# Five instead of eight filler matmuls between the taps' transposes and the first h in a fused convolution and feed-forward kernel

## The chip, the cores and the metric

The kernel runs on one core of a Trainium2 chip. The metric is the device time in microseconds (us), the median of three runs. Engines are named as in the profile: PE is TensorE's matrix multiply and PEld its weight load, DVE is VectorE, ACT is ScalarE, POOL is GpSimd, SP is the engine whose queue issues most of the DMAs (SPq in the rows); ACTq is ScalarE's DMA queue. L12 is line 12 of the kernel.

## The reference

Two layers, each a gated long convolution followed by a feed-forward block, on 2048 rows of 512 values in bfloat16. Cut to what is computed:

```python
def _A_ref(q, k, v, shift_k, ssm_k, ssm_D):      # S = 2048, D = 512, ks = 4
    k_shift = sum over t of k_pad[:, t:t + S, :] * shift_k[:, ks - 1 - t]   # 4 taps
    kv = k_shift * v
    y = causal convolution of kv with ssm_k along S (written with FFTs of length 2 S)
    y = y + kv * ssm_D
    return q * y

def _B_ref(x, w_gate, w_up, w_down):             # F = 1792
    return (silu(x @ w_gate) * (x @ w_up)) @ w_down

x = A_q
for layer in (0, 1):
    x = x + _A_ref(_layernorm(x), A_k, A_v, A_shift_k, A_ssm_k, A_ssm_D)
    x = x + _B_ref(_layernorm(x), B_w_gate, B_w_up, B_w_down)
```

## The kernel before

The 2048 rows are cut into four blocks of 512 rows, and a block into R = 4 residues of 128. The long convolution is done with short spectra made by matmul: a block of the filter (`hn`, the tensor `A_ssm_k`, called h) is transposed on PE into `hs` (`transpose_h`, L489), multiplied by a table of cosines and sines `fwd` (`half`, through `mm` at L323) and copied out of PSUM as `ev` and `G`. A block of k is transposed on PE (`transpose_k`, L378), shifted by the four taps with diagonal matrices `dg` (`shift_mul`, through L323), multiplied by v, and turned into the spectrum `X` (`direct`, L470). Products of spectra come back through a table `inv` (L809). The feed-forward block multiplies by `wg_sb` and `wu_sb` (L323, tile `pf`) and by `wd_sb` (L994, tile `pd`).

Nothing is scheduled at run time. Every operation is added to a plan with an engine, an estimated cost, and the buffers it reads and writes. A table written out by hand, ORDER, gives the one order in which all operations are issued; each engine executes its own instructions in that order. `Plan.order` computes an estimated start and end for each operation from the costs, and the PSUM or SBUF slot of each buffer. PSUM slots come in three rings, `pf` (4 slots), `pc` (2) and `pd` (2). Real waits are semaphores, put in by the framework where a buffer written by one instruction is used by another, or a slot is used again.

`Plan.issue` walks through the order and emits the instructions. Ahead of a PE operation that by the estimate begins over 0.5 us after the PE operation before it, and before 32 us, it emits filler matmuls: `warm` (L1307) multiplies a constant 128x128 matrix of ones by itself n times into a free PSUM slot, and nothing reads the outcome. In the profile they are the tile `wm`. The number is the estimated gap, less an allowance, divided by 0.106 us. There are three such places in the kernel before: 25 fillers at the very start, 8 between the taps' transposes and the transposes of h, and 2 much later, ahead of the spectrum of the second h.

The first operations of PE, in program order, are then:

- 25 fillers into a slot of ring `pf`.
- four tiny transposes of the taps (`turn_taps`, L1173), into a slot of ring `pd`; the first waits for the DMA of `tapR`, issued on ACT's queue (L1107).
- 8 fillers into slot 0 of ring `pf`.
- 16 transposes of h (L489), four for each residue. The first weight load waits for the DMA of `hn`, which is the first on SP's queue (L354); the first transpose itself waits for a semaphore of PE, since it writes the PSUM slot that the last filler wrote.
- 12 transposes of k (L378); the first weight load waits for the DMA of `kn`, the second on SP's queue (L364).
- the first spectrum matmuls on `hs` and `fwd`, and so on.

DVE copies residue 0 of h into `hs`, adding the row `drow` (L502), and residue 1 (L505); ACT copies residues 2 and 3 (L499). Each waits for four of PE's transposes.

Of the kernel before, what the change touches and what calls it, by code (L numbers as in the profile page):

```python
# [140 lines left out]
class Plan:  # L141
# [78 lines left out]
    def issue(self, seq, place, when, warm_until, warm):  # L220
        t, busy = 0.0, {}
        for o in seq:
            start, end = when[o]
            if o.eng == "PE":
                if start < warm_until and start - t > 0.5:
                    for ring, i in [(r, i) for r in ("pf", "pd", "pc") for i in range(self.rings[r])]:
                        if busy.get((ring, i), 0.0) <= t:
                            n = int((start - t - (0.0 if 0.0 < t < 8.0 else 0.3)) / 0.106)
                            if n > 0:
                                warm(ring, i, n)  # L230
                            break
                t = end
            for b in o.bufs:
                if b.t is None:
                    b.slot = place.get(b, 0)
                    b.t = b.make(b.slot)
                if b in place:
                    busy[b.ring, place[b]] = max(when[q][1] for q in b.ops) + 0.2
            o.emit()
# [1101 lines left out]
```

## Time and profile before

| what | us |
|---|---|
| median of three runs (343.62 to 343.71) | 343.68 |
| time of the profiled execution | 343.72 |
| its span, from the first to the last instruction | 341.9 |
| PE busy in the span | 337.6 |
| DVE busy | 282.5 |
| ACT busy | 252.5 |
| POOL busy | 37.0 |

The profiled execution spends 1.8 us outside the span. Times in the rows of the timeline and of the chain are counted from the span's start; a row of the timeline gives start, duration, engine, line, operation and tiles, and how many instructions of one kind in sequence it stands for, with the idle time before them in brackets. The ends of matmuls are modelled, and matmuls overlap, so what one costs PE is read from the distance between starts, not from its duration.

### The profile page before, as it was taken

What the parts mean: (1) busy time and instruction counts of PE and PEld (TensorE: products, weight loads), DVE (VectorE), ACT (ScalarE), POOL (GpSimd) and SP (SyncE); (2) the same over time, 40 slices, a digit from 0 to 9 for tenths busy, and PEclk for the clock granted to TensorE, in tenths of its full rate; (3) what the DMA queues carried; (4) which work ended last, traced back from release to release, by engine and by line L of the source; (5) the groups of instructions that cost most, each with busy time, mean ns of one, the idle gap of its engine ahead of it and who ended that gap; (6) DMA issues with size and microseconds to landing.
All of it is one profiled execution on the core that took longest, in us unless ns stands there. A gap on an engine that the chain in (4) does not pass through costs nothing.

```text
span 341.9 us, 6474 instructions
## 1 busy us (share of the span) xinstructions
PE 337.6 (99%) x2566; PEld 243.4 (71%) x2566; DVE 282.5 (83%) x478; ACT 252.5 (74%) x496; POOL 37.0 (11%) x46
## 2 busy tenths in 40 slices
PE   9999999999999999999999999999999999999996
PEld 7656858668686567768587756768685877777683
DVE  8899999999999999999999999889997433726022
ACT  6999999999977475778999963778665545545451
POOL 4000100102106100103200000101101000001000
PEclk9999999999999999999999999999999999999999
DMA  7999314050325164010110223010102100001011
GB/s 262 342 314 350 55 31 63 0 155 1 34 46 94 31 124 140 3 30 2 33 31 3 48 46 125 0 33 1 33 0 49 32 33 0 15 17 31 17 33 31
DMA packets 42088, 22.95 MB, mean 67 GB/s; under 512 B 33989, under 2 KB 39882, under 8 KB 42058
## 3 DMA queue, kind: packets, MB, share of 16 engines
q1 hardware_dynamic: 41904, 22.49, 26.1%
q8 instruction: 20, 0.33, 0.4%
q14 instruction: 10, 0.08, 0.1%
q10 hardware_dynamic: 154, 0.05, 0.1%
HBM read 12.33 MB, written 2.10 MB: 42 GB/s over the span
## 4 chain that ended last, share of the span: by engine, by line
PE 93%; ACT 3%; DVE 1%; DMA 1%; issue 0%; POOL 0%; POOLq 0%; ACTq 0%
PE pf L323 56%; PE pd L994 27%; PE ps L323 6%; PE ps L470 2%; DMA zT<-z 1%; ACT H L431 1%; PE wm L1307 1%; PE pt L489 1%; ACT Yk L729 1%; ACT ks L526 0%; ACT n L874 0%; DVE bnst L821 0%; ACT Yk L703 0%; PE pt L378 0%; DVE xc L902 0%
## 5 line engine op out<-in xcount | busy, mean ns | idle before, releaser
L323 PE MATMUL pf<-zT,wu_sb 128*128 128x256 bf16 (+1 forms) x872 | 110.0, 275 | 0.4 <-DMA zT<-z 0.3
L323 PE MATMUL pf<-zT,wg_sb 128*128 128x256 bf16 (+1 forms) x872 | 110.3, 276 | 0.0
L994 PE MATMUL pd<-wd_sb,ht 128*128 128x512 bf16 (+1 forms) x462 | 106.2, 373 | 0.0
L323 PEld LDWEIGHTS <-wu_sb 128*128 128x128 bf16 x872 | 85.2, 98 | 19.5 <-DMA zT<-z 0.8
L323 PEld LDWEIGHTS <-wg_sb 128*128 128x128 bf16 x872 | 85.3, 98 | 17.3
L977 ACT CAST ht<-pf 128x512 bf16<-128x512 f32 x112 | 64.8, 590 | 23.7 <-PE pf L323 23.4
L974 ACT ACTIVATE sg<-pf 128x512 bf16<-128x512 f32 x112 | 66.3, 603 | 20.7 <-PE pf L323 17.3
L994 PEld LDWEIGHTS <-ht 128*128 128x128 bf16 x462 | 45.1, 98 | 44.1
L979 DVE TENSOR_TENSOR ht<-ht,sg 128x1024 bf16<-128x1024 bf16 (+1 forms) x61 | 38.8, 640 | 20.4 <-ACT ht L977 14.3
L826 POOL TENSOR_TENSOR rstd<-ve,nhalf 128x2 f32<-128x2 f32 x24 | 25.1, 1046 | 193.1 <-DVE ve L824 193.1
L821 DVE BATCH_NORM_STATS2 bnst<-xc 128x6 f32<-128x512 bf16 x48 | 31.8, 684 | 0.5
L1075 ACT CAST dn<-pd 128x512 bf16<-128x512 f32 x30 | 17.2, 588 | 17.5 <-PE pd L994 17.5
L431 ACT ACTIVATE X<-ps 128x512 bf16<-128x512 f32 x32 | 18.9, 606 | 10.5 <-PE ps L323 10.0
L1078 DVE TENSOR_TENSOR xc<-xc,dn 128x1024 bf16<-128x1024 bf16 x15 | 10.3, 686 | 16.8 <-ACT dn L1075 16.8
L669 DVE TENSOR_TENSOR t<-X,G 128x2048 bf16<-128x2048 bf16 x18 | 21.9, 1217 | 0.1
L665 DVE TENSOR_TENSOR t<-X,G 128x2048 bf16<-128x2048 bf16 x18 | 21.9, 1219 | 0.0
L855 POOL TENSOR_TENSOR rstd<-ve,nhalf 128x2 f32<-128x2 f32 x8 | 8.4, 1048 | 79.3 <-ACT ve L853 79.3
L679 DVE TENSOR_TENSOR Z<-Z,t 128x2048 bf16<-128x2048 bf16 x12 | 14.7, 1221 | 0.3
L677 DVE TENSOR_TENSOR t<-t,t 128x2048 bf16<-128x2048 bf16 x12 | 14.6, 1219 | 0.2
L431 ACT ACTIVATE H<-ps 128x512 bf16<-128x512 f32 x24 | 14.1, 611 | 0.0
L901 DVE TENSOR_TENSOR n<-n,Yk 128x1024 bf16<-128x1024 bf16 x15 | 10.3, 689 | 3.2 <-ACT n L874 1.9
L323 PE MATMUL ps<-hs,fwd 128*128 128x512 bf16 x40 | 12.7, 379 | 0.1
(103 smaller groups left out, 322.4 us busy)
## 6 DMA issues: line engine op xcount, KB each, us to landing
hn<-in_A_ssm_k_dram SPq DMA_DIRECT2D x4, 512.0 KB, 5.9
vt<-in_A_v_dram SPq DMA_DIRECT2D x4, 512.0 KB, 6.4
xc<-in_A_q_dram SPq DMA_DIRECT2D x4, 512.0 KB, 5.3
out_dram<-xc SPq DMA_DIRECT2D x15, 128.0 KB, 1.8
wg_sb<-in_B_w_gate_dram SPq DMA_DIRECT2D x1, 1792.0 KB
wu_sb<-in_B_w_up_dram SPq DMA_DIRECT2D x1, 1792.0 KB, 8.3
wd_sb<-in_B_w_down_dram SPq DMA_DIRECT2D x1, 1280.0 KB, 11.8
kn<-in_A_k_dram SPq DMA_DIRECT2D x1, 512.0 KB, 4.3
```

Source lines behind the costliest of these rows:

```text
L323: nc.tensor.matmul(o, lhsT=lhsT, rhs=rhs, start=(n == 0), stop=(n == len(terms) - 1))
L431: add("ACT", act(D), lambda: nc.scalar.activation(out=view(), in_=ps.t[:], func=ACT.Copy, scale=scale), r=[ps], w=[(buf, keys)], conv=conv)
L665: dve(n * D, lambda t1=t1, part=part: nc.vector.tensor_mul(out=t1.t[:], in0=x.t[:, sl, 0, :], in1=g.t[:, sl, part, :]), [(x, key(slots, (0 ...
L669: dve(n * D, lambda t2=t2, part=part: nc.vector.tensor_mul(out=t2.t[:], in0=x.t[:, sl, 1, :], in1=g.t[:, sl, 1 - part, :]), [(x, key(slots ...
L679: dve(n * D, lambda t1=t1, part=part: nc.vector.tensor_add(out=z.t[:, sl, part, :], in0=z.t[:, sl, part, :], in1=t1.t[:]), [t1], [zk], con ...
L821: add("DVE", 0.6, lambda st=st, i=i: nc.vector.bn_stats(out=st.t[:], in_=xs[c].t[:, i, :]), r=[(xs[c], (i,))], w=[st])
L826: add("POOL", pw, lambda: nc.gpsimd.tensor_tensor(out=rstd.t[:], in0=ve.t[:], in1=nhalf.t[:].to_broadcast((P, n)), op=ALU.pow), r=[ve, nha ...
L974: add("ACT", act(D), lambda ps=ps, sl=sl: nc.scalar.activation(out=sg.t[:, sl], in_=ps.t[:], func=ACT.Silu), r=[ps], w=[(sg, (b,))], due=( ...
L977: add("ACT", act(D), lambda ps=ps, sl=sl: nc.scalar.copy(out=ht.t[:, sl], in_=ps.t[:]), r=[ps], w=[(ht, (b,))], due=(us[0], at, 1.5, "a"))
L979: dve(n * m * W, lambda: nc.vector.tensor_mul(out=ht.t[:], in0=ht.t[:], in1=sg.t[:]), [sg], [ht], due=(us[0], (k + n) / NF, 0.0, "h"))
L994: nc.tensor.matmul((pds[o] if not cs.start else pds[HP]).t[:, cs], lhsT=ht.t[:, q, at, o * P:(o + 1) * P], rhs=wt["d"].t[:, ft, cs], start ...
L1075: add("ACT", act(D), lambda o=o: nc.scalar.copy(out=dn.t[:, o, :], in_=pds[o].t[:]), r=[pds[o]], w=[(dn, (o,))], due=(unit, 1.0, 3.0, "h"))
```

## The change

One constant in `Plan.issue`: where the operation before the gap ended, by the estimate, between 0 and 8 us, the allowance taken off the gap is 0.35 us instead of nothing. Only one of the three places falls in that range, the one between the taps' transposes and the first transpose of h. There the number of fillers goes from 8 to 5. In program order PE loses three weight loads and three matmuls of L1307 there; every other instruction of PE, and all those of DVE, ACT, POOL and SP, stand in the same order with the same waits. No buffer changes its slot.

```diff
@@ Plan.issue
                 if start < warm_until and start - t > 0.5:
                     for ring, i in [(r, i) for r in ("pf", "pd", "pc") for i in range(self.rings[r])]:
                         if busy.get((ring, i), 0.0) <= t:
-                            n = int((start - t - (0.0 if 0.0 < t < 8.0 else 0.3)) / 0.106)
+                            n = int((start - t - (0.35 if 0.0 < t < 8.0 else 0.3)) / 0.106)
                             if n > 0:
                                 warm(ring, i, n)
                             break
```

## The prediction

> **What bounds the kernel now.** I read the page first: its busy times, then the chain that ended last.
>
> ```profile
> span 341.9 us, 6474 instructions
> PE 337.6 (99%) x2566; PEld 243.4 (71%) x2566; DVE 282.5 (83%) x478; ACT 252.5 (74%) x496; POOL 37.0 (11%) x46
> PE 93%; ACT 3%; DVE 1%; DMA 1%; issue 0%; POOL 0%; POOLq 0%; ACTq 0%
> ```
>
> PE is busy nearly all the time and carries 93% of the chain. So any time that PE gains at the start can reach the end, if nothing between is tied to something that does not move. Next, the chain in order of time, cut to the start and to the places where it leaves PE (start, length, what):
>
> ```profile
> 0.76 2.83 PE wm L1307 x25
> 3.58 0.22 PE pt L1173 x4
> 3.81 0.98 PE wm L1307 x8
> 4.83 1.32 PE pt L489 x16
> 6.15 0.67 PE pt L378 x12
> ...
> 20.14 1.74 PE ps L470 x8
> 21.91 0.60 ACT X L431
> ...
> 31.91 0.62 ACT zT L940
> 32.58 1.91 PE pf L323 x16
> ...
> 261.15 4.00 DMA zT<-z
> 265.20 8.91 PE pf L323 x80
> ```
>
> The eight fillers lie on the chain, and the first transpose of h follows them with no DMA between. That is the important point: in this execution PE made h wait for the fillers, not the fillers for h. Whether h was there sooner is read from the start of its DMA, and from the distance of issue to landing:
>
> ```profile
> 0.72 0.46 SPq L354 DMA_DIRECT2D hn<-in_A_ssm_k_dram  x1
> hn<-in_A_ssm_k_dram SPq DMA_DIRECT2D x1, 512.0 KB, 3.5
> 1.24 0.49 SPq L364 DMA_DIRECT2D kn<-in_A_k_dram  x1
> kn<-in_A_k_dram SPq DMA_DIRECT2D x1, 512.0 KB, 4.3
> ```
>
> h landed at 0.72 + 3.5 = 4.22 us, give or take 0.05 for the rounding, and k at 1.24 + 4.3 = 5.54. The first transpose of h started at 4.83, 0.6 us after h was there.
>
> **The change step by step.** The timeline of PE around the place, with rows that narrow windows gave (start, length, count from that start on):
>
> ```profile
> 3.74 1.03 PE L1307 MATMUL wm<-const-bfloat16-1.0 128*128 128x128 bf16 x8
> 3.82 0.63 PE L1307 MATMUL wm<-const-bfloat16-1.0 128*128 128x128 bf16 x4
> 4.14 0.63 PE L1307 MATMUL wm<-const-bfloat16-1.0 128*128 128x128 bf16 x4
> 4.46 0.31 PE L1307 MATMUL wm<-const-bfloat16-1.0 128*128 128x128 bf16 x1
> 4.46 0.15 PEld L489 LDWEIGHTS <-hn 128*128 128x128 bf16 x1
> 4.83 1.32 PE L489 MATMUL pt<-ident,hn 128*128 128x128 bf16 x16
> 5.32 0.45 PE L489 MATMUL pt<-ident,hn 128*128 128x128 bf16 x4
> 5.42 0.39 PE L489 MATMUL pt<-ident,hn 128*128 128x128 bf16 x4
> 5.49 0.44 PE L489 MATMUL pt<-ident,hn 128*128 128x128 bf16 x5
> 5.54 0.39 PE L489 MATMUL pt<-ident,hn 128*128 128x128 bf16 x4
> 5.99 0.83 PE L378 MATMUL pt<-ident,kn 128*128 128x128 bf16 x12
> ```
>
> *What goes.* The second filler starts at 3.82 and the eighth at 4.46: (4.46 - 3.82) / 6 = 0.107 us each. Three fewer free 3 x 0.107 = 0.32 us. The fifth starts at 4.14 and, as long as the eighth, ends at 4.14 + 0.31 = 4.45. Before, the eighth ended at 4.46 + 0.31 = 4.77 and the first transpose began 0.06 later, which is its wait for PE's own semaphore. So now it can begin at 4.45 + 0.06 = 4.51.
>
> *What takes its place.* The weight load of h, which followed the eighth filler's without a wait, would follow the fifth's at 4.14 and now meet the DMA. In the chain, DMA zT ended at 261.15 + 4.00 = 265.15 and PE started at 265.20: 0.05 us from landing to start. So the load starts at about 4.22 + 0.05 = 4.27 (4.32 with the rounding) and takes 0.15: done at 4.42 to 4.47, just inside 4.51. The cover is thus 0.2 us if the matmul needs only the start of its load, and about 0.05 if it needs the end. Should h land later than this, each 0.1 us of it costs 0.1 us of the start, until at 0.32 us nothing is left of the gain.
>
> *What three fewer fillers are worth.* Not 0.32. The starts of the transposes go 5.32, 5.42, 5.49, 5.54: the distance falls from 0.107 to 0.056 at about 5.45. That is the clock of the array opening (the page's row of granted clock does not show it; the distances do). With the start at 4.51, three more transposes are done when the clock opens, and at the full clock three cost 3 x 0.056 = 0.17 us. If the clock opens at the same moment, or after the same number of matmuls of this size (25 fillers, 8 fillers and 7 transposes before; 25, 5 and 10 after, both ending at 5.42), all later work on PE begins 0.17 us sooner: the transposes of k at 5.82 instead of 5.99. k has landed by then (5.54 + 0.05 = 5.59), so this does not stop it: a margin of 0.23 us.
>
> [...]
>
> *What the other engines make of it.* The copies of h wait for PE, with all their idle time put down to the transposes:
>
> ```profile
> 5.45 0.42 DVE L502 TENSOR_TENSOR hs<-pt,drow 128x512 bf16<-128x512 bf16 x1 [0.42 <-PE pt L489]
> 5.74 1.07 ACT L499 COPY hs<-pt 128x512 bf16<-128x512 bf16 x2 [0.40 <-PE pt L489]
> ```
>
> DVE's first copy needs the fourth transpose, which comes 0.32 us sooner, and may start at 5.13; by its bracket DVE was idle from 5.45 - 0.42 = 5.03. ACT's needs the eighth, at 5.21 instead of 5.49, and may start at about 5.5; it was idle from 5.74 - 0.40 = 5.34. So both gain 0.2 us or more, and will not hold PE back. Of the queues, SP and POOL are moved past nothing; no DMA is issued sooner or later because of the fillers in this stretch.
>
> *Does it reach the end?* The table of stretches (us, then PE busy of it):
>
> ```profile
> 5.40:21.90 16.50, 16.50 (x159) 10.84 (x156) 15.23 (x32) 14.91 (x32) 2.56 (x5) 1.00 1.07 315
> 32.60:254.00 221.40, 221.40 (x1643) 160.74 (x1643) 215.13 (x326) 181.12 (x360) 26.44 (x23) 1.00 0.22 47
> ```
>
> PE has no idle time from 5.4 to 21.9, so 0.17 us is carried whole to 21.9. There the chain goes over to ACT: `X` at 21.91 begins just as the last matmul of 20.14 + 1.74 = 21.88 ends, so ACT's stretch to 32.5 begins 0.17 sooner too. From 32.6 to 254 PE is full again, and the transposing DMA at 261.15 follows from PE's and ACT's work, not from a fixed time. I find nothing on the chain after 6 us that stands still. What DMA brings by a fixed time (v, the weights, the tables) does not appear on it.
>
> The sum: the profiled execution 343.72 - 0.17 = 343.55; its time was 0.04 above the median of the runs, so about 343.5 for a median. The bounds of this term: nothing, if h lands 0.3 us later in other executions or a later stage takes the gain back; 0.32, if the earlier start of DVE and ACT counts rather than PE's. I take 0.17, since the two windows with no idle PE say that PE sets the pace. A change of 0.2%, 0.7 us, is about what a measurement of this kernel can tell from no change; 0.17 is far below.
>
> **The rivals.**
>
> *The clock opens later (slower).* The mechanism sits at 5.45 us. It decides if transposes count for less than fillers, and if the work seen until then is near the least that opens the clock. Before, 33 fillers had run by then; after, 30. If only work other than transposes counts, three matmuls of that size are missing, and the next to count are the spectrum matmuls that follow 16 + 12 transposes: at 0.107 us those 28 take 3.0 us from 4.51 on, so to 7.5, and one spectrum matmul of 512 columns (four times 0.107) makes up the rest: the clock opens at about 7.9. From 5.45 to 7.9 PE runs at half the pace and loses 2.45 / 2 = 1.2 us; less the 0.17 gained, +1.05: 344.7. The least is a delay of only the three fillers' 0.32 us, half of it lost, which just eats the gain. The most is that the whole waiting starts again at 5.45 for as long as it took from the first filler to the opening, 5.45 - 0.76 = 4.7 us: 2.35 lost, +2.2, 345.9. Since PE has no idle time until 21.9, nothing would hide it. Against it: the opening came in the middle of the transposes, 0.6 us after PE had gone over to them, which looks as if they count. For it: a window of fixed length could show the same. [...] Chance 0.30.
>
> *The gain does not arrive.* h lands later without the profiler or by chance, or one of the waits between 21.9 and 32.6 takes the 0.17 us back, since ACT and DVE are nearly full there. Then 343.7. For it: the cover of 0.05 to 0.2 us at the landing of h is thin. Against it: the chain. Chance 0.15.
>
> *More than forecast.* If the clock opened with the first transposes, PE would be at k's transposes at 5.59, where the landing of k stops it: 5.99 - 5.59 = 0.40 sooner, 343.3. Nothing speaks for an earlier opening. Beyond that no row has a gain of 0.7 us. Chance 0.10 in all, of which I leave 0.06 for a gain above 0.2% by something that these rows do not show.
>
> **How the numbers follow.** The forecast, 343.4 to 343.6, has 0.45, and with it goes the most likely value, 343.5. Within 0.2% lie the forecast, the case without gain and the smaller part of the third rival: 0.45 + 0.15 + 0.04 = 0.64. Slower is the first rival, 0.30. The range begins at 343.3 (the third rival's price) and must reach into the slower case to leave out only 2 in 10: to 344.9, which takes in 344.7 and leaves out the repeats of a whole wait. Its own range without the slower case would be 343.3 to 343.7.
>
> **What would show it.** In the profile of the changed kernel: five `wm` in the second group, the first transpose of h at 4.5, with its load at about 4.3 after a wait for the DMA; the step from 0.107 to 0.056 at 5.4 to 5.5, in the tenth or eleventh transpose; k's transposes at 5.8; and `X` on the chain at 21.7. I am wrong if the starts still lie 0.107 apart after 5.6, if h's load comes later than 4.5, or if the difference at 21.9 is not that at 5.99.

## The result and the profile after

The changed kernel took 342.98 us (median of ten runs, 342.88 to 343.64) against 343.97 for the kernel before in the same runs. The ratio is 0.9974, with a 95% interval of 0.9966 to 0.9982: faster by 0.6 to 1.2 us, where 0.17 was forecast. The profiled execution took 343.52 us with a span of 341.7, against 343.72 and 341.9 before. That is a gain of only 0.2, since these two executions started differently, as will be seen.

The start first. Three views of the changed kernel's PE: the weight loads of h, and the starts around the opening of the clock (start, length, count from there on).

```profile
4.46 0.78 PEld L489 LDWEIGHTS <-hn 128*128 128x128 bf16 x8 [0.28 <-DMA hn<-in_A_ssm_k_dram]
4.50 0.69 PE L489 MATMUL pt<-ident,hn 128*128 128x128 bf16 x5
...
6.27 0.47 PE L378 MATMUL pt<-ident,kn 128*128 128x128 bf16 x4
6.38 0.41 PE L378 MATMUL pt<-ident,kn 128*128 128x128 bf16 x4
6.46 0.39 PE L378 MATMUL pt<-ident,kn 128*128 128x128 bf16 x4
6.52 0.39 PE L378 MATMUL pt<-ident,kn 128*128 128x128 bf16 x4
```

The first transpose of h begins at 4.50, as forecast, its load after a wait for the DMA. But the starts are 0.11 us apart until 6.38 and 0.06 from 6.46 on: the clock opened at about 6.4, not 5.45, one microsecond later. So the work at 32 us is not ahead but behind: the first `pf` matmul stands at 32.88, against 32.58 on the chain before. Yet the execution ended 0.2 us sooner. So about 0.5 us must have been gained after 32 us. The chain in order of time, in the changed kernel, at the place where before it came from ACT, DVE and POOL to the transposing DMA at 261.15:

```profile
263.88 1.29 PE pd L994 x6
265.18 8.73 PE pf L323 x80
```

Now the chain stays on PE. (It counts the `pd` matmuls up to their modelled end at 265.18; the next matmuls start before that.) When `pf` really starts is in the timeline of PE, before and then after:

```profile
264.29 0.59 PE L994 MATMUL pd<-wd_sb,ht 128*128 128x512 bf16 x2
265.20 0.61 PE L323 MATMUL pf<-zT,wu_sb 128*128 128x256 bf16 x4 [0.32 <-DMA zT<-z]
```

```profile
264.37 0.81 PE L994 MATMUL pd<-wd_sb,ht 128*128 128x512 bf16 x3
265.01 0.82 PE L323 MATMUL pf<-zT,wu_sb 128*128 128x256 bf16 x6
```

Before, `pf` began at 265.20 because it had to wait for `zT`; now it begins at 265.01, without a wait, though PE was 0.3 us behind at 32 us. These 0.19 us are the 0.2 us by which the execution ended sooner.

The instructions on the tile `zT` between 261.0 and 262.2 us, first before, then after:

```profile
L908 SPq DMA_TRANSPOSE zT<-z x2: 1190/1224/1259, 259.9 to 261.2; - x2
DMA to landing us min/median/max: 2.4/3.2/4.0
```

```profile
L908 SPq DMA_TRANSPOSE zT<-z x2: 1198/1228/1257, 260.2 to 261.4; - x2
DMA to landing us min/median/max: 2.4/2.4/2.5
```

The same two DMAs: the second took 4.0 us to land before and 2.5 after. What lengthened it is read from the DMA queues, in narrow windows (queue and kind, packets that start in the window, MB, share of 16 engines; the share sets the packet's whole time against the window and says little here). Before, from 263.0 to 263.2, beside packets of the data queue q1:

```profile
q8 instruction: 1, 0.02, 32.3%
```

From 263.3 to 264.1 no packet starts at all, and then, from 264.1 to 264.2, the whole answer on queues is:

```profile
q1 hardware_dynamic: 2, 0.00, 2.8%
```

In the changed kernel from 262.0 to 265.0, the whole answer on queues, and then from 265.0 to 265.2:

```profile
q1 hardware_dynamic: 721, 0.25, 35.4%
...
q8 instruction: 1, 0.02, 30.0%
```

Queue q8 carries instructions. The page has 20 of its packets over the whole span, 0.33 MB, about one in 17 us. I take them to be PE's: the page has 5132 weight loads and matmuls for PE, a good 256 for each of the 20, and under 500 instructions for any other engine. In the trace before, one packet, 16 KB, ran from 263.09 to 264.12, while the second transposing DMA was under way: 15 of its 16 parts landed by 263.63, the last at 265.15. The two small packets above start at 264.11 and 264.12, as the instruction packet ends; 30 such packets had started by 263.3, two for each of the 15 parts that had landed. So the last part stood behind the instruction packet. After the change this packet comes at 265.14, when `zT` has landed (263.93). That gave theory F: the change takes six instructions out of PE's program, so that the fetches fall at other places in the work, and one of them no longer meets the one DMA that PE waits for. The rival, theory S, is that of the prediction: the gain comes from the earlier start.

### The profile page after: what moved, and what is told of

Its sections match the earlier page's. It is cut to its first block, busy times and chain, and to the rows that moved or that the text cites. A ratio compares the mean times of both kernels' runs of the same rounds, so it can differ in the third digit from the quotient of the medians.

```text
span 341.7 us, 6468 instructions
## 1 busy us (share of the span) xinstructions
PE 337.7 (99%) x2563; PEld 243.7 (71%) x2563; DVE 282.4 (83%) x478; ACT 252.5 (74%) x496; POOL 37.0 (11%) x46
## 4 chain that ended last, share of the span: by engine, by line
PE 96%; ACT 3%; issue 0%; ACTq 0%
PE pf L323 57%; PE pd L994 28%; PE ps L323 6%; PE ps L470 2%; ACT H L431 1%; PE wm L1307 1%; PE pt L489 1%; ACT Yk L729 1%; ACT ks L526 0%; ACT n L874 0%; PE pt L378 0%; ACT zT L940 0%; ACT X L431 0%; ACT xc L1052 0%; PE pt L1173 0%
```

## The experiments

The helper that emits the fillers was given a list of widths, so that the number of fillers, their columns and the number of instructions could be set apart:

```diff
     def warm(ring, slot, n):
-        t = psp.tile([P, P], F32, name="wm", tag=f"{ring}{slot}")
-        for _ in range(n):
-            nc.tensor.matmul(t[:], lhsT=ones, rhs=ones, start=True, stop=True)
+        t = psp.tile([P, 512], F32, name="wm", tag=f"{ring}{slot}")
+        for w in fillers.pop(0):
+            if w == 4:
+                nc.tensor.matmul(t[:, 0:4], lhsT=ones[0:4, :], rhs=ones[0:4, 0:4], start=True, stop=True)
+            else:
+                nc.tensor.matmul(t[:, 0:w], lhsT=ones, rhs=wide[:, 0:w], start=True, stop=True)
```

Here `wide` is the same constant one, 512 columns wide. Each experiment is one list for the three groups, written short here.

**Eight fillers, three pairs fewer.**

```diff
+    fillers = [[128] * 19 + [256] * 3, [128] * 8, [128] * 2]
```

> Eight fillers stay ahead of h, but PE has three pairs of weight load and matmul fewer, as the changed kernel: in the first group 19 fillers of 128 columns and 3 of 256 take the place of 25 of 128, the same columns in all. Theory S (start): the gain of the change comes from the earlier first transpose of h; then this kernel is as the kernel before, ratio 1.000. Theory F (fetch): most of it comes from where PE's 16 KB instruction fetches fall; three pairs fewer move the fetch that fell at 263.09 us on the second zT transpose behind it; then zT lands 2.5 us after its issue, not 4.0, PE loses nothing at 265 us, and the kernel is 0.5 us faster than before, ratio about 0.9985.

Measured: 343.33 us against 344.11, ratio 0.9977 (0.9968 to 0.9986). The whole gain of the change is there, without the change. Its instruction packet comes at 265.51, and its two transposes land undisturbed:

```profile
DMA to landing us min/median/max: 2.4/2.5/2.5
```

**Five fillers, as many instructions as before.**

```diff
+    fillers = [[128] * 25 + [4] * 3, [128] * 5, [128] * 2]
```

> Five fillers ahead of h as in the changed kernel, but three tiny pairs (4 columns) are put at the end of the first group, where PE waits 0.14 us for the taps' DMA anyway, so PE has as many instructions as before. Theory S: as the changed kernel, ratio 0.997 to 0.9995. Theory F: the fetch falls on the second zT transpose again, which lands 4 us after its issue; only the 0.17 us of the earlier start is left, ratio about 0.9995.

Measured: 344.00 us against 344.11, ratio 0.9996 (0.9987 to 1.0005): the change, and no gain that can be told from none. Its `zT`, then the DMA queues from 263.0 to 263.2 with the instruction packet, then PE's waits from 262 to 267 (in total, times, longest):

```profile
DMA to landing us min/median/max: 2.4/3.3/4.1
```

```profile
q8 instruction: 1, 0.02, 34.9%
```

```profile
PE pf L323 <- DMA zT<-z: 0.5, 1, 0.5
```

These two decide between S and F: the number of instructions does nearly all. What the number of fillers ahead of h does by itself is too small to be told from nothing; by the interval it is a gain of at most 0.13%, 0.45 us.

**Both kernels once more.**

> The changed kernel once more, for its scatter and a second profile. Ratio 0.9966 to 0.9982 as measured. Theory F: no instruction fetch while the zT transposes of 260 to 264 us run, no wait at 265. The moment at which the distance of PE's starts falls from 0.107 to 0.056 us (6.4 us in the first profile, 5.45 in that of before) differs again, and the time goes with half of that difference.

> The kernel before once more, for a second profile. Theory F: an instruction fetch of PE between 261 and 265 us, the second zT transpose lands about 4 us after its issue, and PE waits about 0.5 us at 265. If zT lands after 2.5 us and the time is as ever, theory F falls. The clock's opening may come at another moment than 5.45 us.

Measured: the changed kernel 343.34 us against 344.11 in the median; its ratio is 0.9992 (0.9974 to 1.0010), because two of its twelve executions, at 345.20 and 346.51, pull it up and widen it. I have no trace of those two. So by its ratio this repeat alone does not show the gain; the medians differ by 0.77 us, against 0.99 in the first measurement. The kernel before was run once with a profile, 343.68 us. In the profiles the second `zT` landed 2.5 us after its issue in the changed kernel, with the packet at 264.78, and 4.2 us after in the kernel before, with the packet at 262.82. So the meeting is no accident of one execution. In both other traces in which the packet meets `zT` the picture is that of the first: 15 parts land by 263.3 or 263.6, the last by 265.07 or 265.29, and two small packets start just as the instruction packet ends.

**Six pairs fewer, twelve pairs more.** Is fewer instructions simply better?

```diff
+    fillers = [[128] * 13 + [256] * 6, [128] * 8, [128] * 2]
```

> Eight fillers ahead of h, and six pairs fewer on PE: in the first group 13 fillers of 128 and 6 of 256 columns, the same columns in all. Theory F: PE's fetch falls 12 instructions later in the work than before, after the zT transposes of 260 to 264 us; zT lands 2.5 us after its issue, no wait at 265; ratio about 0.998, as with three pairs fewer. Theory S: 1.000. A third reading, that each pair less is worth something by itself, would have twice the gain of three pairs, 0.996.

Measured: 343.49 us against 344.07, ratio 0.9978 (0.9969 to 0.9986), as with three pairs fewer: the gain does not grow with the pairs. Then the other way, with 24 instructions more (a width of 64 also has 64 rows of output):

```diff
+    fillers = [[64] * 24 + [128] * 13, [128] * 8, [128] * 2]
```

> Eight fillers ahead of h, and twelve pairs more on PE: in the first group 12 of the 25 fillers are each cut in two of 64 columns. Theory F: the fetch that fell at 263 us falls 24 instructions earlier in the work, at 259.5 to 261.5 us, ahead of the packets of the second zT transpose; then zT lands in time and the kernel is faster than before by up to 0.5 us though it has more instructions (ratio 0.9985 to 0.9995), unless the fetch still meets the packets of the transposes (261.1 to 263.6), which the trace will tell. Theory S, or that fewer instructions are better by themselves: 1.000 or slower.

Measured: 343.28 us against 344.07, ratio 0.9981 (0.9972 to 0.9990). More instructions, and faster than before. The packet, which the DMA queues show from 260.1 to 260.3, began at 260.20 and took 0.95 us, so it is over before the first of the transposing DMAs, issued at 260.7 and 261.9, moves data, at 261.84. Their landing, then the queue's row:

```profile
DMA to landing us min/median/max: 2.4/2.5/2.5
```

```profile
q8 instruction: 1, 0.02, 29.5%
```

**What the fillers are worth.**

```diff
+    fillers = [[128] * 25 + [4] * 5, [], [128] * 2]
```

> No fillers between the taps' transposes and h; five tiny pairs at the end of the first group, so PE has as many instructions as the changed kernel. h's transposes then begin when h lands (4.25 to 4.8 us), as with five fillers or up to 0.2 us sooner, but PE stands idle for 0.6 to 1 us before. If the fillers only fill, ratio as the changed kernel's, 0.9977, or 0.0003 less. If the idle time makes the clock open a window later in more of the executions, 0.998 to 1.001. In either case zT lands in time at 264 us, by theory F.

Measured: 344.46 us against 344.07, ratio 0.9999 (0.9985 to 1.0013). The times fall in two groups: four from 342.95 to 343.53, eight from 344.29 to 345.10. The profiled execution is of the first group, and its `zT` landed in 2.5 us. The instruction count is that of the changed kernel, so leaving the fillers out seems to cost about 1.4 us in two thirds of the executions. (The interval lies above that of the changed kernel's first measurement, but overlaps that of its repeat.) That size suits a clock that opens later, as the prediction's first rival priced it (+1.05), but no trace of the second group shows it: argued, not shown.

**Without the late fillers.**

```diff
+    fillers = [[128] * 25 + [4] * 2, [128] * 5, []]
```

> The changed kernel without the two fillers at 22 us, whose last one makes the next matmul wait 0.22 us for its PSUM slot; two tiny pairs at the end of the first group keep the number of instructions, so the fetches stay where they are in the changed kernel. If PE sets the pace at 22 us, 0.2 to 0.3 us faster than the changed kernel, ratio about 0.9970 to the kernel before. If ACT and DVE set it from 21.9 us on, as the chain says, no gain: 0.9977.

Measured: 342.98 us in the median of five runs, ratio 0.9966 (0.9954 to 0.9979). It is the lowest ratio of all, but its interval overlaps that of the changed kernel. From the first spectrum matmul of `ps<-vt,fwd` to the first of `pf`, the trace has 13.61 to 32.28, 18.67 us, against 14.21 to 32.88, also 18.67, in the changed kernel. So the late fillers cost nothing on the path, as the second reading expected. No kernel here is shown to beat the changed one.

All executions with a trace, side by side. The fifth column is the second `zT` from issue to landing; the last is the span less the start of the first `pf` matmul.

| kernel | PE instructions against before | instruction packet, us | k lands / its transposes start | `zT` | first `pf` | rest |
|---|---|---|---|---|---|---|
| before | 0 | 263.09 | 5.54 / 5.99 | 4.0 | 32.58 | 309.3 |
| before, again | 0 | 262.82 | 5.63 / 5.68 | 4.2 | 32.28 | 309.6 |
| five, plus 3 pairs | 0 | 263.12 | 5.94 / 5.98 | 4.1 | 32.57 | 309.5 |
| after | -6 | 265.14 | 5.70 / 6.17 | 2.5 | 32.88 | 308.8 |
| after, again | -6 | 264.78 | 5.87 / 5.91 | 2.5 | 32.50 | 308.9 |
| eight, less 3 pairs | -6 | 265.51 | 6.04 / 6.09 | 2.5 | 32.69 | 308.9 |
| eight, less 6 pairs | -12 | 265.05 | 6.07 / 6.12 | 2.5 | 32.72 | 308.9 |
| eight, plus 12 pairs | +24 | 260.20 | 5.83 / 6.63 | 2.5 | 33.32 | 308.9 |
| no fillers before h | -6 | 264.94 | 6.23 / 6.28 | 2.5 | 32.88 | 308.8 |
| five, no late fillers | -6 | 265.15 | 5.63 / 5.67 | 2.5 | 32.28 | 308.9 |

The last column has two values: 308.8 to 308.9 where the packet misses `zT`, 309.3 to 309.6 where it meets it. Taken apart, this stretch differs at one step alone. From the first `pf` matmul to the last `pd` matmul ahead of those that wait for `zT` it is 231.9 us in all ten traces, and from the first `pf` matmul behind `zT` to the end 76.7 to 76.8. Between these two matmuls lie 0.21 to 0.22 us in the seven traces where the packet misses, and 0.70, 0.91 and 0.84 in the three where it meets. So the meeting costs 0.5 to 0.7 us, and that is the effect of the change, as far as these traces show one.

## Why the prediction was wrong

**The start of h: right in the profile, of little use.** The five fillers, the wait of the load for the DMA and the start at 4.5 came as forecast. The cover was thinner than thought: h landed at 4.24 in the profile that I had, and the other nine traces have it at 4.30 to 4.80. In the changed kernel's first profile the load began at 4.46, not 4.27, so only 0.04 us of cover was left; in the second one h itself set the start, at 4.64.

**The margin at k's landing: wrong.** The step was "k has landed by then", with "a margin of 0.23 us", from a landing at 5.54. That was the earliest of the ten. In seven of them k's transposes start 0.04 to 0.05 us after k's landing: the DMA sets the start, not PE, and neither five nor eight fillers matter. The kernel before, again, starts them at 5.68 after such a wait, and the row of the changed kernel, again, is:

```profile
5.91 0.84 PE L378 MATMUL pt<-ident,kn 128*128 128x128 bf16 x12 [0.19 <-DMA kn<-in_A_k_dram]
```

In the three others (before, after, and twelve pairs more) PE came to them later, held up by the eight fillers or by the slow clock. From the start of k's transposes to the first `pf` it is 26.6 to 26.7 us in all ten; the step that carries the start through to 32 us thus held.

**The opening of the clock: right that it need not move with the fillers, wrong that it stands still.** The kernel before opened it at 5.45 in one trace and by about 3.8 in the other, where the eight fillers took 0.64 us instead of 1.03:

```profile
3.74 0.64 PE L1307 MATMUL wm<-const-bfloat16-1.0 128*128 128x128 bf16 x8
```

The changed kernel opened it at 6.4 in one trace; in the other its five fillers took 0.55 us, against 0.72 in the first, so it was opening among them. In both first profiles PE's first filler starts at 0.76 us, so the opening is not a fixed time behind it; over these four traces it scatters by over 2.5 us. The record of the granted clock kept with the ten traces has the openings from 3.67 to 6.84 us (5.43 and 6.43 in the two first profiles). In it the full clock lasts 337.92 us in eight traces and 334.51 in two, 3.41 apart; the two lengths are 99 and 98 times 3.41. The three runs ahead of the prediction, within 0.09 us, showed no such scatter. Ten runs of the same kernel spread from 343.62 to 344.57: three were too few. The late opening of the first rival did come in the profile of the changed kernel, by about 1 us, but it is a scatter of both kernels. That transposes count for less than fillers, on which that rival and its +1.05 rest, no run shows: in both first profiles the starts fall from 0.107 to 0.056 us amid transposes, the eighth in the kernel before and the twentieth in the changed one.

**"I find nothing on the chain after 6 us that stands still": the step that failed.** Removing instructions was priced as the time that they take on PE. What they also do, to move a later fetch of instructions against the work (from about 263 us to about 265), had no term. The trace had two rows for it. The chain that I quoted has the DMA of `zT` with 4.00 us, where the median of the two was 3.2 and the first took 2.4; I read this row as PE's and ACT's work passed on and did not ask why it was so long. And the page lists q8 among the queues, which I did not look at. The mis-sized term is the stretch from 32.6 us to the end: forecast 0, measured -0.5 to -0.7. That the change came out faster, as forecast, is luck: the gain that the runs show comes from this stretch, and none is shown from the start.

**The sum.** The fetch gives 0.5 to 0.7 us of the 0.6 to 1.2 measured. What may be left is within the interval. Whether five fillers instead of eight give up to 0.17 us more stays open: 0.9996 (0.9987 to 1.0005) with the fetch as before holds both that and nothing.

**Also open**: why six instructions moved the packet by about 2 us, when three pairs of PE in that stretch take 3 x 0.22 = 0.65 us. The traces show when the packet runs, not what asks for it. Nor do they show why the last part landed 1.0 us after its small packets had started, where the others took about 0.4.

## What to carry to other kernels

When a DMA on the chain takes longer than its twins (here 4.0 us against 2.4), look in its window for what else ran on the DMA engines, the instruction queue among it, before taking its length for given. In this kernel each edit that changed the number of PE's instructions moved the fetch at 263 us; so an edit of a few instructions, with an effect of a few tenths of a per cent, needs a control with as many instructions and without the edit, or its ratio may not be that of the edit. And take landings and the clock's opening from several traces: a margin of 0.2 us in one execution may not exist in the next.

## What was not expected of the hardware

One packet of instructions, which I take to be PE's, 16 KB in 1.0 us, held up one of the sixteen parts of a transposing DMA: 15 had landed by 263.63, the last came at 265.15, 1.5 us later. With the eight fillers kept, kernels with 6 or 12 instructions fewer, and one with 24 more, were all faster than the kernel before, by 0.19 to 0.23%. And in ten executions of nearly the same program the first block of h landed from 4.24 to 4.80 us and that of k from 5.54 to 6.23, with the same DMA issues at the same times.
